# The last tile of a sorted expert layer: 32 rows with float32 weights in column tiles, and a result buffer of its own

## The chip, the core and the metric

One core of a Trainium2 chip runs the program. The metric is device time in microseconds (us) of one execution; lower is better. The engines are named as the profile names them: PE (TensorE), DVE (VectorE), ACT (ScalarE), POOL (GpSimd) and SP (SyncE, which only starts transfers).

## What is computed

Attention over 4 batches, 12 heads, 448 positions and a head width of 64, all float32; its output, 1792 tokens of 768 numbers, goes through a layer of eight experts, of which each token takes the one with the highest logit:

```python
attn_out = _attn_ref(**attn_kwargs)                # causal softmax attention
x = attn_out.transpose(0, 2, 1, 3).reshape(1792, 768)
...
expert_idx = np.argmax(logits, axis=1)             # cosine of x and expert_emb, over tau
gate_w = probs[np.arange(N), expert_idx]
for e in range(8):
    mask = expert_idx == e
    h = np.maximum(x[mask] @ w1[e], 0.0)           # 768 -> 1024
    out[mask] = gate_w[mask, None] * (h @ w2[e])   # 1024 -> 768
```

## The kernel before, in words

The attention runs over 24 pairs of heads in an order written out by hand (`ORDER`, a list of step names with the pair's number). Its last part also sorts the tokens by expert and prepares the expert layer: how many tiles there are, which expert each tile has, which rows it holds.

**Tiles.** The tokens of an expert are cut into tiles of at most 128 rows. The expert with the most tokens comes first, the others follow in their order. With these inputs the experts have 1, 319, 229, 126, 542, 464, 87 and 24 tokens, which makes 18 tiles, numbered 0 to 17. Tiles 0 to 4 are expert 4's, tile 5 expert 0's, 6 to 8 expert 1's, 9 and 10 expert 2's, 11 expert 3's, 12 to 15 expert 5's, tile 16 the 87 rows of expert 6, and tile 17 the 24 rows of expert 7. The program holds 21 tiles (`NT`); from tile 14 (`TMIN`) on, each tile is inside a runtime `If(nt > t)` (L1006, `nt` being the number of tiles), whose `Else` is `last(t - 1)`.

**Flags.** Small integers that a kernel reads into registers at run time tell each engine which form of a tile to run. `small[t]` (read by `load_few`, L574, tested in L584) is 1 for at most 64 rows, 2 for a larger tile of the same expert as the one before, 0 for a larger tile of a new expert. `mt` holds each tile's expert, then a flag that is 1 if the expert changes at this tile (`cc`, read in `val`, L531), then `nt`. Steps U0 to U5 and H0 to H2 (L839 to L876) make them on one partition, among the last steps of `ORDER`.

**Products.** A product in float32 is made of rounded parts: weights are split into a high part (ACT cast, L905) and a low part (DVE subtraction, L906), and so is the token side; a whole tile takes three matmuls for each block (L681 to L683), a tile of at most 64 rows, with high and low token parts side by side in the 128 columns, two (L690, L691). `r1` and `r2` are the weights as loaded, `h1`, `l1`, `h2`, `l2` their parts.

**Order within a tile** (`body(t)`): product 1 of tile t; the split of the next tile's w1 where the expert changes; the loads of w1 for tile t+2; the hidden values of t out of PSUM (`hiddens`); the flags of t+1; tile t+1's tokens turned (`turn_x`, six PE transposes, L623) and split (`next_x`); the gather of tile t+3; product 2 of tile t-1, with the turn of t's hidden values (`turn_h`, eight PE transposes, L632) between its k = 4 and k = 5; the split of w2 for t (L905, L906); `split_h(t)` (the ReLU and the split of the turned values, DVE's part in L670); `finish(t - 1)`; the loads of w2 for t+1. `last(t)` does product 2 of the last tile, two halves of 384 columns one after the other, and `finish`.

**finish** multiplies the two halves by the gate, one half on ACT (L755), one on DVE (L758), into one buffer `ob`, and POOL scatters its rows to the output with an indirect DMA (L766). In a tile of at most 64 rows ACT scales the lower half of the PSUM (L749, by `gu`, a copy of the gates on partitions 64 to 127, made in `upper`), and DVE adds the upper half into `ob` (L752). `ob` is one buffer for all tiles.

**Before the first `body`** come `loads(2, 1)`, which reads flags of tile 2 on SP, ACT, DVE and POOL, and `gate_parts`: ACT takes a square root (L952), DVE refines it (L298 and on), ACT takes an exponential (L962), and POOL makes `Mg` (L975), from which PE makes the gates in tile 1 (`gates`, L986).

The logits use column tiles already: `LT` steps (L449) run three matmuls of 32 columns each (`tile_position`), on 448 columns of data in float32.

Of the kernel before, what the change touches and what calls it, by code (L numbers as in the profile page):

```python
# [18 lines left out]
P = 128  # L19
# [14 lines left out]
K0 = [1, 2, 3, 4, 5, 6, 7, 0]  # L34

# [93 lines left out]
def attn_moe(tc, qk, vv, emb, tau, w1, w2, out):  # L129
# [3 lines left out]
    with ExitStack() as ctx:  # L133
# [51 lines left out]
        junk = T("junk", [DM], BF16)  # L185
# [30 lines left out]
        hh1, ob, xt1, hh0 = (cut(fa, P, n, at=at + o) for n, o in ((F, 0), (DM, F), (DM, F + DM), (F, F + 2 * DM)))  # L216
# [65 lines left out]
        gt, gu = T("gt", [NT], parts=P), T("gu", [NT], parts=P)  # L282
# [228 lines left out]
        for c in range(NC):  # L511
            step(f"Q{c}", LAST)(lambda p, c=c: ac.activation(
                junk, Xs[p // PB % 2][:, c], AF.Square, accum_out=n2[:, NC * (p // PB) + c : NC * (p // PB) + c + 1]))
# [59 lines left out]
        def load_few(t, engines):  # L573
            return nc.values_load(small[0:1, t : t + 1], engines=engines, min_val=0, max_val=2,  # L574
                                  skip_runtime_bounds_check_because="made on chip within these bounds")

        def branch(flag, small_, whole_, light_=None):

            def rest():
                with tc.If(flag > 1) as c:  # L580
                    light_()
                with c.Else():
                    whole_()
            with tc.If(flag == 1) as c:  # L584
                small_()
            with c.Else():
                rest() if light_ else whole_()

        def either(t, engine, small_, whole_, light_=None):

            if t < 2:
                whole_()
            else:
                branch(few[t][engine], small_, whole_, light_)
# [33 lines left out]
        def turn_h(t):  # L628

            def rows():  # L630
                for k in range(KF):
                    pe.transpose(pf[t][k // 4][:, k % 4], hb[t][:, k * P : k * P + P], idt)  # L632
            if t < 2:
                rows()
            else:
                with tc.If(few[t][ET.PE] < 2):
                    rows()

        def turn_light(t):

            blocks = hb[t].rearrange("p (k j c) -> p k j c", k=KF, j=4)

            def light_():
                for q in range(0, P, 32):
                    for j in range(4):
                        v.transpose(xk[32 * j : 32 * j + 32, :, q : q + 32], blocks[q : q + 32, :, j])  # L646
            if t > 1:
                with tc.If(few[t][ET.DVE] > 1):
                    light_()

        def next_x(t, px):
            h, l = ([x[:, 3 * a : 3 * a + 3] for a in range(2)] for x in xs[t][1:])
            for a in range(2):
                ac.copy(h[a], px[a])

            def small_():
                for a in range(2):
                    v.tensor_tensor(h[a][:, :, 64:], px[a][:, :, 0:64], h[a][:, :, 0:64], op=ALU.subtract)

            def whole_():  # L660
                for a in range(2):
                    v.tensor_tensor(l[a], px[a], h[a], op=ALU.subtract)
            either(t, ET.DVE, small_, whole_)

        def split_h(t):
            x, h, l = hs[t]
            pts = [(slice(4 * a, 4 * a + 4), pf[t][a]) for a in range(2)]

            def low(out, x, h):
                v.scalar_tensor_tensor(out, x, 0.0, h, op0=ALU.max, op1=ALU.subtract)  # L670
            either(t, ET.Activation, lambda: [ac.activation(h[:, o, 0:64], pt[:, :, 0:64], AF.Relu) for o, pt in pts],
                   lambda: [ac.activation(h[:, o], pt, AF.Relu) for o, pt in pts], lambda: ac.activation(h, xk, AF.Relu))
            either(t, ET.DVE, lambda: [low(h[:, o, 64:], pt[:, :, 0:64], h[:, o, 0:64]) for o, pt in pts],
                   lambda: [low(l[:, o], pt, h[:, o]) for o, pt in pts], lambda: low(l, xk, h))
# [24 lines left out]
        def product2(t, acc, ks=range(KF), js=(0, 1)):  # L699
            either(t, ET.PE, lambda: small_product(acc, hs[t][1], h2, l2, ks, KF, 384, js),  # L700
                   lambda: product(acc, *hs[t][1:], h2, l2, ks, (K0[0], K0[-1]) if t == 0 else (0, KF - 1), 384, js))

# [24 lines left out]
        def hiddens(t, acc):  # L727

            hs[t] = hb[t] = hh_ring.next()

            def low(j):
                return hb[t][0:64, 512 * j : 512 * j + 512]

            either(t, ET.Activation, lambda: [ac.copy(low(j), acc[j][64:128]) for j in range(2)],
                   lambda: [hidden(t, acc, j) for j in range(2)])
            either(t, ET.DVE, lambda: [v.tensor_tensor(low(j), acc[j][0:64], low(j), op=ALU.add) for j in range(2)],
                   lambda: v.memset(apart, 0.0))
# [3 lines left out]
        def finish(t, acc, ends):  # L741
            def half(j):
# [16 lines left out]

            if ends and t > 1:  # L760
                branch(load_few(t, [ET.DVE, ET.Activation]), lambda: [f(j) for j in range(2) for f in (small_a, small_v)],
                       lambda: (whole_a(), whole_v()))
# [77 lines left out]
        ef, ef2 = T("ef", [NT], parts=1), T("ef2", [NT], parts=1)  # L840
# [17 lines left out]
        same, sa = T("same", [NT], parts=1), T("sa", [NT], parts=1)  # L858

        @step("H0", END)  # L860
        def _(p):
            v.tensor_scalar(sm, us, 1.0 / SKIP, None, ALU.mult)
            v.memset(same, 0.0)

        @step("H1", END)
        def _(p):
            st["f"] = end_ring.next()[:, :NT]
            pe.matmul(st["f"], idt[:, 64:65].broadcast_to([P, P]), sm, start=True, stop=True)
# [39 lines left out]
        def body(t):  # L908
# [6 lines left out]
            if t + 1 < NT:  # L915
                with tc.If(cc[t + 1] != 0):
# [15 lines left out]
            if t > 1:  # L932
                with tc.If(cc[t] != 0):
# [3 lines left out]
            if t > 1:  # L937
                with tc.If(cc[t] != 0):  # L938
# [3 lines left out]
        def last(t):  # L942
            acc = [a[:, :384] for a in acc1]
            for j in range(2):
                product2(t, acc, js=[j])
# [31 lines left out]
        def upper():  # L977

            f = pt_ring.next()[:, :NT]
# [69 lines left out]
```

## Time and profile before

| | |
|---|---|
| median of 3 runs | 509.47 us (509.18 to 509.82) |
| the profiled execution's own time | 508.89 us |
| its span | 507.0 us |
| mean granted clock of PE | 0.994 of full speed |
| PE busy | 490.0 us, 97% of the span |
| DVE / ACT / POOL busy | 349.2 / 337.1 / 72.3 us |

The span is what the profiler sees between the first and the last event; the profiled execution's own time is 1.89 us longer. Attention fills the span up to about 200 us, tiles 0 and 1 and the preparation of the flags and gates the time to about 222 us, the other tiles the rest. Two matmul rows that follow each other overlap in the records, so what a stretch of PE work takes is read from the start of its first row to the start of the next stretch's, not from the rows' durations. The products of tile 17 are the rows of L690 and L691 from 475.82 us (product 1) and from 492.15 us (product 2).

### The profile page before, as it was taken

The page shows a single profiled execution, that of the slowest core. Times are in us where ns is not written, and L with a number is a line of the kernel's source. Part 1 is how long each engine was busy: PE and PEld are TensorE (multiplying, and loading weights), DVE is VectorE, ACT ScalarE, POOL GpSimd, SP SyncE. Part 2 cuts the span into 40 slices and gives each one's busy share as a digit, 9 for nine tenths or more (in the row PEclk, how much of TensorE's full clock was granted, in tenths as well). Part 3 has the DMA queues.
Part 4 walks back from the last instruction along what each step waited for, and adds up shares of the span by engine and source line. Part 5 has one row for each costly group of instructions (what it writes and reads, how often), then busy time and mean ns, then how long its engine had stood idle before and what let it go on. Part 6 is the DMA issues. An engine that isn't in the chain of part 4 may idle for free. (4 is left out here: it accounts for less than half of the span.)

```text
span 507.0 us, 10532 instructions
## 1 busy us (share of the span) xinstructions
PE 490.0 (97%) x3120; PEld 391.1 (77%) x3120; DVE 349.2 (69%) x948; ACT 337.1 (66%) x811; POOL 72.3 (14%) x89
## 2 busy tenths in 40 slices
PE   8999999999999999999999999999999999999992
PEld 5656566666656557888889898899889988988992
DVE  4866585676668568845486986837988554788871
ACT  5999999999999994721255962617676621256660
POOL 2000000000000351230112022200221020012111
PEclk9999999999999999999999999999999999999997
DMA  8232353173235971311449775368677312567831
GB/s 246 67 109 86 126 172 110 58 217 109 63 116 172 343 240 56 95 56 40 174 171 382 262 240 184 141 239 347 255 265 267 129 64 78 237 238 294 274 123 35
DMA packets 27368, 87.19 MB, mean 172 GB/s; under 512 B 2694, under 2 KB 3142, under 8 KB 27280
## 3 DMA queue, kind: packets, MB, share of 16 engines
q1 hardware_dynamic: 24160, 72.38, 41.3%
q0 software_dynamic: 3120, 13.77, 7.6%
q8 instruction: 39, 0.64, 0.5%
q14 instruction: 49, 0.40, 0.2%
HBM read 144.33 MB, written 12.58 MB: 309 GB/s over the span
## 5 line engine op out<-in xcount | busy, mean ns | idle before, releaser
L381 ACT ACTIVATE aq<-aq,mx 112x112 f32<-112x112 f32 (+3 forms) x192 | 99.8, 525 | 4.6 <-DVE mx L376 4.6
L376 DVE CUSTOM_DVE_ANT_0 aq<-bank,ar 112x112 f32<-112x112 f32 (+1 forms) x192 | 76.1, 441 | 30.5 <-PE bank L371 30.1
L399 PE MATMUL bank<-idt,aq 112*112 112x112 f32 x480 | 62.3, 265 | 1.1 <-DVE ap L404 0.4
L399 PEld LDWEIGHTS bank<-idt,aq 112*112 112x112 f32 x480 | 46.7, 133 | 19.5 <-ACT ap L404 6.8
L371 PE MATMUL bank<-ak 64*112 64x112 f32 (+3 forms) x384 | 56.6, 419 | 0.8 <-DVE mx L376 0.8
L725 ACT COPY fa<-bank 128x512 f32<-128x512 f32 x28 | 15.2, 587 | 56.6 <-PE bank L681 48.0
L766 POOL DMA_INDIRECT out_dram<-fa,isx x18 | 26.4, 1469 | 183.5 <-DVEq L938 60.0
L404 ACT COPY ap<-bank 112x336 f32<-112x336 f32 (+2 forms) x118 | 50.4, 457 | 2.7 <-PE bank L399 0.8
L412 PE MATMUL bank<-ap 112*64 112x448 f32 (+3 forms) x384 | 51.7, 407 | 0.0
L906 DVE TENSOR_TENSOR wl<-fa,wh 128x1024 fp32r<-128x1024 f32 x42 | 48.4, 1219 | 3.6 <-PE bank L682 2.1
L646 DVE STREAM_TRANSPOSE turned<-fa 32x256 f32<-32x256 f32 x112 | 48.8, 436 | 1.5
L412 PEld LDWEIGHTS bank<-ap 112*64 112x64 f32 x384 | 25.0, 136 | 29.9 <-issue 17.6
L905 ACT CAST wh<-fa 128x1024 fp32r<-128x1024 f32 x42 | 40.7, 1047 | 4.4 <-PE bank L683 2.0
L371 PEld LDWEIGHTS bank<-ak 64*112 64x112 f32 x384 | 27.4, 175 | 13.0 <-issue 3.5
L381 ACT ACTIVATION_READ_ACCUMULATOR aq<-aq,mx 112x1 f32 x192 | 37.1, 193 | 0.0
L565 POOL DMA_INDIRECT fa<-xd,ig x21 | 23.5, 1117 | 75.9 <-PE bank L623 54.6
L681 PE MATMUL bank<-wh,akr 128*128 128x512 f32 x84 | 32.9, 391 | 0.0
L683 PE MATMUL bank<-wh,akr 128*128 128x512 f32 x84 | 32.9, 391 | 0.0
L683 PE MATMUL bank<-wh,apr 128*128 128x512 f32 x84 | 32.8, 391 | 0.0
L682 PE MATMUL bank<-wl,aor 128*128 128x512 f32 x84 | 32.8, 390 | 0.0
L682 PE MATMUL bank<-wl,akr 128*128 128x512 f32 x84 | 32.8, 390 | 0.0
L681 PE MATMUL bank<-wh,aor 128*128 128x512 f32 x84 | 32.8, 390 | 0.0
(292 smaller groups left out, 1061.1 us busy)
## 6 DMA issues: line engine op xcount, KB each, us to landing
fa<-in_w_dram SPq DMA_DIRECT2D x76, 768.0 KB
fa<-in_w_dram SPq DMA_DIRECT2D x54, 1024.0 KB
ak<-in_qk_dram SPq DMA_DIRECT2D x24, 448.0 KB
ap<-in_vv_dram SPq DMA_DIRECT2D x24, 224.0 KB
xd<-fa SPq DMA_DIRECT2D x3, 1344.0 KB
fa<-in_w_dram SPq DMA_DIRECT2D x6, 512.0 KB
xd<-fa SPq DMA_DIRECT2D x1, 1120.0 KB
fa<-xd,ig POOLq DMA_INDIRECT x21, 6.4
```

The lines of the kernel that those rows point to most:

```text
L371: pe.matmul(o, raws[p % 4][rows, 0, CP * i : CP * i + CP], raws[p % 4][rows, 1, :n], start=True, stop=True, tile_position=(D * h, 0), skip ...
L376: v.tensor_tensor_reduce(out=Ps[p % 2][i, h], in0=st.pop(("sp", p, i, h)), in1=mask[i], scale=-0.125, scalar=3e38, op0=ALU.add, op1=ALU.mi ...
L381: ac.activation(x, x, AF.Exp, bias=mxs[p % 3][:, h, i : i + 1], scale=-1.0, accum_out=sums[p % 3][:, h, i : i + 1])
L399: pe.transpose(t[:, x, c], Ps[p % 2][i, h][:, c * CP : c * CP + CP], idt[:CP, :CP])
L404: (ac.copy if q == "A" and (p, n) not in ONV else v.tensor_copy)(o, st.pop(("pt", p, n)))
L412: pe.matmul(bo[64 * h : 64 * h + 64, CP * c : S], vts[p % 4][:, c, 64 * h : 64 * h + 64], PTs[p % 2][:, h, 4 * c : 3 * c + NC], start=c == ...
L646: v.transpose(xk[32 * j : 32 * j + 32, :, q : q + 32], blocks[q : q + 32, :, j])
L681: pe.matmul(acc[j], xh[:, k], wh[k][:, o], start=k == ends[0], stop=False)
L682: pe.matmul(acc[j], xh[:, k], wl[k][:, o], start=False, stop=False)
L683: pe.matmul(acc[j], xl[:, k], wh[k][:, o], start=False, stop=k == ends[1])
L905: ac.copy(h[k], r[:, k])
L906: v.tensor_tensor(l[k], r[:, k], h[k], op=ALU.subtract)
```

## The change

The flag `small` gets a value 3: the last tile, if its expert is new and it has at most 32 rows. Such a tile's weights are not split; both products use them as loaded, in float32, with the token side's 32 columns as stationary operand and the weight's columns in four quarters, each on 32 PE columns of its own. `cc` gets a value 2 for it, by which the splits are skipped and the loads are not. The last tile writes its result into the next buffer of the ring for gathered tokens, whatever its form. `junk` goes; its steps write into a part of another buffer. `hq` and `gq` are new, `xq` is the old `en`.

```diff
-        junk = T("junk", [DM], BF16)
...
+        gt, gu, gq = T("gt", [NT], parts=P), T("gu", [NT], parts=P), T("gq", [NT], parts=P)
+        hq, xq = T("hq", [KF, QR], parts=P), en.rearrange("p k r -> p k r")
...
         def turn_h(t):
...
-                with tc.If(few[t][ET.PE] < 2):
+                with tc.If(few[t][ET.PE] < 2) as c:
                     rows()
+                if t >= TMIN:
+                    with c.Else():
+                        with tc.If(few[t][ET.PE] > 2):
+                            rows(KF // NQ)
...
         def next_x(t, px):
...
+            def tiny_():
+                for a in range(2):
+                    v.tensor_copy(xq[:, 3 * a : 3 * a + 3], px[a][:, :, 0:QR])
+            either(t, ET.DVE, small_, whole_, tiny_=tiny_)
...
         def split_h(t):
...
+                   lambda: ac.activation(hq.rearrange("p (q b) r -> p b q r", q=NQ),
+                                         pf[t][0][:, 0 : KF // NQ].rearrange("p b (q r) -> p b q r", q=NQ), AF.Relu))
...
+                   lambda: v.memset(apart, 0.0))
...
+        def tiny_product(acc, x, w, nk, n):
+
+            for k in range(nk):
+                for q in range(NQ):
+                    pe.matmul(acc[0][QR * q : QR * q + QR, :n], x[:, k], w[:, k, n * q : n * q + n], start=k == 0,
+                              stop=k == nk - 1, tile_position=(0, QR * q), skip_group_check=True)
...
         def product1(t, acc):
             either(t, ET.PE, lambda: small_product(acc, xs[t][1], h1, l1, range(KD), KD, 512),
-                   lambda: product(acc, *xs[t][1:], h1, l1, range(KD), (0, KD - 1), 512))
+                   lambda: product(acc, *xs[t][1:], h1, l1, range(KD), (0, KD - 1), 512),
+                   tiny_=lambda: tiny_product(acc, xq, r1, KD, F // NQ))
...
+            either(t, ET.PE, small_, whole_, tiny_=lambda: tiny_product(acc, hq, r2, KF, DM // NQ))
...
         def finish(t, acc, ends):
+            ob = xt_ring.next() if ends else obs
+
...
+            def quarters(qs, f):
+                n = DM // NQ
+                for q in qs:
+                    rows = slice(QR * q, QR * q + QR)
+                    f(ob[0:QR, n * q : n * q + n], acc[0][rows, :n], gq[rows, t : t + 1])
+
+            def tiny_():
+                quarters((0, 1), lambda o, x, s: ac.activation(o, x, AF.Copy, scale=s))
+                quarters((2, 3), lambda o, x, s: v.tensor_scalar(o, x, s, None, ALU.mult))
...
         @step("U5", END)
         def _(p):
-            v.tensor_tensor(mt[:, NT + 1 : 2 * NT], ef[:, 1:NT], ef[:, 0 : NT - 1], op=ALU.not_equal)
-            v.tensor_copy(mt[:, 2 * NT : 2 * NT + 1], ct[0:1, E - 1 : E])
+            nt = ct[0:1, E - 1 : E]
+            v.tensor_tensor(ch[:, 1:], ef[:, 1:NT], ef[:, 0 : NT - 1], op=ALU.not_equal)
+            v.scalar_tensor_tensor(ch, i21[0:1], nt, ch, op0=ALU.is_lt, op1=ALU.mult)
+            v.tensor_copy(mt[:, NT + 1 : 2 * NT], ch[:, 1:])
+            v.tensor_copy(mt[:, 2 * NT : 2 * NT + 1], nt)
+            v.tensor_scalar(lt, i21[0:1], 1.0, nt, ALU.add, ALU.is_equal)
...
         @step("H2", END)
         def _(p):
-            f = st["f"]
-            v.tensor_tensor(same[:, 1:], ef[:, 1:NT], ef[:, 0 : NT - 1], op=ALU.is_equal)
-            v.tensor_tensor(sa, f[0:1], same, op=ALU.mult)
-            v.tensor_tensor(same, same, sa, op=ALU.subtract)
-            v.scalar_tensor_tensor(small, same, 2.0, f[0:1], op0=ALU.mult, op1=ALU.add)
+            f, q = (st["f"][0:1, n * NT : n * NT + NT] for n in range(2))
+            v.tensor_tensor(lt, lt, q, op=ALU.mult)
+            v.tensor_scalar(sa, ch, -1.0, 1.0, ALU.mult, ALU.add)
+            v.scalar_tensor_tensor(sa, f, 0.0, sa, op0=ALU.is_equal, op1=ALU.mult)
+            v.tensor_tensor(sa, sa, lt, op=ALU.add)
+            v.scalar_tensor_tensor(small, sa, 2.0, f, op0=ALU.mult, op1=ALU.add)
+            v.tensor_tensor(mt[:, NT + 1 : 2 * NT], ch[:, 1:], lt[:, 1:], op=ALU.add)
...
-                cc[t] = val(NT + t, 1, [ET.SP, ET.Activation, ET.DVE, ET.Pool])
+                cc[t] = val(NT + t, 2, [ET.SP, ET.Activation, ET.DVE, ET.Pool])
...
         def body(t):
...
-                with tc.If(cc[t + 1] != 0):
+                with tc.If(cc[t + 1] == 1):
                     split_w(r1, h1, l1, range(KD))
...
-                with tc.If(cc[t] != 0):
+                with tc.If(cc[t] == 1):
                     split_w(r2, h2, l2, range(6))
...
         def upper():
...
+            for q in range(NQ):
+                pe.matmul(fq[QR * q : QR * q + QR], idt[:, 0:QR], gt, start=True, stop=True, tile_position=(0, QR * q),
+                          skip_group_check=True)
+            v.tensor_copy(gq, fq)
```

`branch` and `either` get a fourth form (tested by `flag > 2`, only for tiles from 14 on), H0 has a multiplication in place of a memset, H1 a second small matmul, `hiddens` a form in which ACT copies 128 by 256 values, and both halves of product 2 in `last` come under one test instead of two.

## Rows read from the trace of the kernel before

**Rows 1.** The page's first part: busy time and share of the span, by engine.
```profile
PE 490.0 (97%) x3120; PEld 391.1 (77%) x3120; DVE 349.2 (69%) x948; ACT 337.1 (66%) x811; POOL 72.3 (14%) x89
```
**Rows 2.** Stretches of the end: length, busy time by engine, granted clock, DMA share, GB/s.
```profile
491.40:498.20 6.80, 5.96 (x32) 5.51 (x32) 3.19 (x6) 2.33 (x4) 1.82 (x1) 1.00 0.17 55
498.20:507.00 8.80, 0.00 (x0) 0.00 (x0) 1.13 (x2) 0.58 (x1) 1.00 (x1) 0.65 0.03 11
```
**Rows 3.** Waits of PE from 222 to 507 us: total, times, longest.
```profile
PE bank L690 <- DVE aor L670: 0.8, 1, 0.8
```
**Rows 4.** Timeline of PE, tiles 16 and 17: start, duration, instruction, idle time before it.
```profile
475.82 0.39 PE L690 MATMUL bank<-wh,aor 128*128 128x512 f32 x1
...
481.30 0.82 PE L623 MATMUL bank<-idt,fa 128*128 128x128 f32 x6
...
487.17 1.04 PE L632 MATMUL bank<-idt,fa 128*128 128x128 f32 x8
487.96 0.42 PE L681 MATMUL bank<-apr,arr 128*128 128x384 f32 x1
...
492.15 0.41 PE L690 MATMUL bank<-arr,aor 128*128 128x384 f32 x1 [0.79 <-DVE aor L670]
```
**Rows 5.** Timeline of DVE, the two calls of finish and what stands before the first.
```profile
491.58 0.75 DVE L670 SCALAR_TENSOR_TENSOR aor<-bank,aor 128x256 fp32r<-128x256 f32 x2
492.24 0.61 DVE L758 TENSOR_SCALAR fa<-bank,gt 128x384 f32<-128x384 f32 x1
...
499.85 1.13 DVE L752 SCALAR_TENSOR_TENSOR fa<-bank,gt,fa 64x384 f32<-64x384 f32 x2 [5.26 <-DMA out_dram<-fa,isx]
```
**Rows 6.** Timeline of POOL: the scatters of tiles 16 and 17.
```profile
493.66 1.82 POOL L766 DMA_INDIRECT out_dram<-fa,isx  x1 [10.30 <-ACT apr L905]
501.79 1.00 POOL L766 DMA_INDIRECT out_dram<-fa,isx  x1 [6.32 <-POOLq L1006]
```
**Rows 7.** The line of the scatters, 470 to 507 us: durations in ns, first and last start.
```profile
L766 POOLq EVENT_SEMAPHORE  x3: 2014/6475/6782, 471.8 to 499.0; - x3
...
DMA to landing us min/median/max: 2.4/5.3/7.1
```
**Rows 8.** Column tiles in the attention: PE's timeline, and one line's groups.
```profile
101.11 0.95 PE L449 MATMUL bank<-ao,en 128*32 128x448 f32 x6
101.99 0.31 PE L399 MATMUL bank<-idt,aq 112*112 112x112 f32 x1
...
L449 PEld LDWEIGHTS bank<-ao,en x48: 106/108/109, 33.0 to 189.4; 128*32 128x32 f32 x48
```
**Rows 9.** Jumps of the sequencers by line, 485 to 495 us (L584: from 200 us).
```profile
L1006 PEldq COMPARE_BRANCH  x1: 3292/3292/3292, 488.1 to 488.1; - x1
L584 PEldq COMPARE_BRANCH  x38: 63/208/352, 222.4 to 478.6; - x38
...
L1006 ACTq COMPARE_BRANCH  x1: 50/50/50, 491.6 to 491.6; - x1
L574 ACTq TENSOR_LOAD <-small x1: 277/277/277, 494.8 to 494.8; - x1
```
**Rows 10.** The flags and the gates, 209 to 221 us: a flag load by line, then timelines.
```profile
L531 ACTq TENSOR_LOAD <-mt x1: 467/467/467, 209.4 to 209.4; - x1
...
210.23 1.28 ACT L952 ACT_TABLE_LOAD   x1 [0.34 <-issue]
...
212.03 0.17 DVE L876 SCALAR_TENSOR_TENSOR small<-same,bank 1x21 int32<-1x21 f32 x1
212.74 0.17 DVE L298 TENSOR_SCALAR t<-t 112x16 f32<-112x16 f32 x1 [0.55 <-DVE small L876]
...
216.75 2.48 POOL L975 TENSOR_TENSOR Mg<-M,g 112x336 f16<-112x336 f16 x3 [6.20 <-DVE g L969]
...
220.30 0.67 PE L986 MATMUL bank<-Mg,turned 112*128 112x63 f16 x16
```
**Rows 11.** The line of the weight loads on SP, about 480 us: the last load for tile 17.
```profile
L893 SPq DMA_DIRECT2D fa<-in_w_dram x1: 372/372/372, 480.0 to 480.0; - x1
```

More of the change, by code (lines that the diff above doesn't have):

```diff
@@ L34 @@
 K0 = [1, 2, 3, 4, 5, 6, 7, 0]
+QR = 32
+NQ = P // QR
 ORDER = """
@@ L573, in load_few, with branch @@
         def load_few(t, engines):
-            return nc.values_load(small[0:1, t : t + 1], engines=engines, min_val=0, max_val=2,
+            return nc.values_load(small[0:1, t : t + 1], engines=engines, min_val=0, max_val=3,
                                   skip_runtime_bounds_check_because="made on chip within these bounds")
-        def branch(flag, small_, whole_, light_=None):
+        def branch(flag, small_, whole_, light_=None, tiny_=None):
             def rest():
+                if not light_:
+                    return whole_()
                 with tc.If(flag > 1) as c:
@@ L583, in rest, with more @@
                     whole_()
+            def more():
+                if not tiny_:
+                    return rest()
+                with tc.If(flag > 2) as c:
+                    tiny_()
+                with c.Else():
+                    rest()
             with tc.If(flag == 1) as c:
@@ L586, in branch, with either @@
             with c.Else():
-                rest() if light_ else whole_()
-        def either(t, engine, small_, whole_, light_=None):
+                more()
+        def either(t, engine, small_, whole_, light_=None, tiny_=None):
             if t < 2:
@@ L593, in either @@
             else:
-                branch(few[t][engine], small_, whole_, light_)
+                branch(few[t][engine], small_, whole_, light_, tiny_ if t >= TMIN else None)
         def xT(t, a):
@@ L628, in turn_h, with rows @@
         def turn_h(t):
-            def rows():
-                for k in range(KF):
+            def rows(n=KF):
+                for k in range(n):
                     pe.transpose(pf[t][k // 4][:, k % 4], hb[t][:, k * P : k * P + P], idt)
@@ L647, in turn_light @@
             if t > 1:
-                with tc.If(few[t][ET.DVE] > 1):
+                with tc.If(few[t][ET.DVE] == 2):
                     light_()
@@ L734, in hiddens @@
             either(t, ET.Activation, lambda: [ac.copy(low(j), acc[j][64:128]) for j in range(2)],
-                   lambda: [hidden(t, acc, j) for j in range(2)])
+                   lambda: [hidden(t, acc, j) for j in range(2)],
+                   tiny_=lambda: ac.copy(hb[t][:, : F // NQ], acc[0][:, : F // NQ]))
             either(t, ET.DVE, lambda: [v.tensor_tensor(low(j), acc[j][0:64], low(j), op=ALU.add) for j in range(2)],
@@ L862, in _ @@
             v.tensor_scalar(sm, us, 1.0 / SKIP, None, ALU.mult)
-            v.memset(same, 0.0)
+            v.tensor_tensor(lt, lt, ch, op=ALU.mult)
         @step("H1", END)
         def _(p):
-            st["f"] = end_ring.next()[:, :NT]
-            pe.matmul(st["f"], idt[:, 64:65].broadcast_to([P, P]), sm, start=True, stop=True)
+            st["f"] = end_ring.next()
+            for n, row in enumerate((64, QR)):
+                pe.matmul(st["f"][:, n * NT : n * NT + NT], idt[:, row : row + 1].broadcast_to([P, P]), sm, start=True,
+                          stop=True, skip_group_check=True)
         @step("H2", END)
         def _(p):
-            f = st["f"]
-            v.tensor_tensor(same[:, 1:], ef[:, 1:NT], ef[:, 0 : NT - 1], op=ALU.is_equal)
-            v.tensor_tensor(sa, f[0:1], same, op=ALU.mult)
-            v.tensor_tensor(same, same, sa, op=ALU.subtract)
-            v.scalar_tensor_tensor(small, same, 2.0, f[0:1], op0=ALU.mult, op1=ALU.add)
+            f, q = (st["f"][0:1, n * NT : n * NT + NT] for n in range(2))
[5 more added lines that the diff above has]
+            v.tensor_tensor(mt[:, NT + 1 : 2 * NT], ch[:, 1:], lt[:, 1:], op=ALU.add)
         for _ in range(16):
@@ L943, in last @@
             acc = [a[:, :384] for a in acc1]
-            for j in range(2):
-                product2(t, acc, js=[j])
+            product2(t, acc)
             finish(t, acc, True)
```

34 lines of the change are left out of this document (20 added, 14 removed).

## Prediction

> **What bounds the kernel now.** The page's first part comes first: PE is busy 97% of the span [rows 1]. Such a share says nothing yet of a change at the end, so the second view is the table of stretches: PE is full up to 491.4, has an idle part up to 498.2, and in the last 8.8 us no instruction at all; there it is two DVE calls, one ACT call, one POOL call and waiting [rows 2]. The third is the waits of PE from 222 us on: the only one worth naming is the 0.8 us on DVE before product 2 of the last tile [rows 3]. So from 222 to 492 us every us of PE work, and every us by which PE starts late, goes straight to the end. The timelines then give the end as a chain. PE's last product of tile 16 gives way at 491.36 (0.79 before 492.15 [rows 4]); DVE does the second half of `finish(16)` at 492.24, 0.88 late because L670 sits ahead of it [rows 5]; POOL starts the scatter at 493.66, 0.81 after DVE's end at 492.85 [rows 5, 6]; it lands 5.3 us later, at 499.0, which is when the last semaphore wait of the scatters' line begins [rows 7]. DVE waits for that landing, 5.26 us, because `ob` is one buffer, and runs only from 499.85 to 500.98 [rows 5]; the last scatter starts at 501.79 and lands 2.4 us later, near 504.2 [rows 6, 7]; the span ends 2.8 us after. Product 2 of tile 17, over by 498.2 [rows 2], isn't in this chain: the first scatter's landing is.
>
> The same rows show that POOL itself waits for the scatter before: its three semaphore waits of 2.0 to 6.8 us stand in the line of the scatters, and one begins at the landing just named [rows 7]. A second buffer takes away DVE's wait, but I keep POOL's: the two scatters write the same output.
>
> **Part by part, PE before the end.** Product 1 of tile 17 takes 475.82 to 481.30, 5.48 us for 24 matmuls of 512 columns [rows 4]. It becomes 24 float32 matmuls of 256 columns on four column tiles. The nearest rows are three column tiles of 448 columns in float32: six instructions for three calls, so two passes, and 101.11 to 101.99 = 0.88 us for both [rows 8]. If the three ran one after another, each call of 448 columns would have 0.29 us for two passes, less than one pass of a whole-array product of 512 columns scaled to 448 (5.48 / 24 x 448 / 512 = 0.20, twice is 0.40). So tiles do run side by side. Per column and pass it is at most 0.88 / 896 = 0.98 ns; part of that is the start of a stretch, and I take 0.85 ns and 0.24 us once. Six k by two passes by 256 columns by 0.85 ns, and 0.24, is about 2.83 us. The gain is **2.65 us**. The bounds: 0.75 ns (gain 2.9), and four tiles in place of three at a proportional price (4/3 x 0.98 ns x 3072 = 4.0, gain 1.5).
>
> `turn_h(17)` does two transposes in place of eight; eight take 487.17 to 487.96, 0.79 us [rows 4], so **0.59 us** go. Both lie in PE's full stretch. Product 2 of tile 16 then ends at 491.36 - 3.24 = 488.12.
>
> **The end.** With no split for tile 17, neither L670's part nor a weight split stands ahead of `finish(16)` on DVE: it starts at about 488.2 and ends at 488.81 (0.61 [rows 5]), POOL starts at 489.62, the scatter lands at 494.94 (5.3 [rows 7]). That is 4.04 earlier. POOL then starts the last scatter 0.81 after that landing, at 495.75, if its data are there; before, the DVE call and its waits stood between (501.79 - 499.0 = 2.8 from landing to start), so another 2.0 go. 495.75 + 2.45 + 2.76 gives 500.96 in place of 507.0: **6.05 us**.
>
> The data must be there by 494.9. Product 2 of tile 17 is 8 k x 2 passes x 192 columns at 0.85 ns, 2.6 and start-up, 2.7 us; its 64 matmuls with as many weight loads issue in that time if they go as fast as the 16 of L986, 0.67 us for 16, 42 ns each [rows 10]. It starts after PE's jump to the `Else`. That jump took 3.29 us, where 38 others of L584 took 0.06 to 0.35 [rows 9]; PE's sequencer reached it 3.3 us ahead of the engine, so it was hidden, and it moves with the work: start near 488.65, end 491.35. ACT's own jump lasted from 491.6 to the flag's load at 494.8 [rows 9], 3.2 us. It moves by PE's 3.2, to 488.4, and is over near 491.6; DVE's, begun when its part of `finish(16)` ends at 488.81, would by the same length be over near 492.0. With the flag's load and two quarters on each engine (half of a 0.61 each, say 0.3) the data are there near 493.0 to 493.3. The slack is **1.6 us**; in it lie the last product's size, the six transposes fewer and the ReLU, which move nothing.
>
> The Trainium skill ("Runtime: NRT & Kernel Launch", section "Instruction fetch mechanics") says that a taken branch whose target lies outside the window of two pages forces a fetch by DMA before execution goes on; the 3.29 us against 0.06 to 0.35 agree. By that page a fourth form in the code adds targets, and a second such jump could stand on the last chain; it is rival B.
>
> **The price, at the flags.** H2 now ends with a write to the `cc` flags, which ACT reads for tile 2 before its square root. Before, that load ran at 209.4, while DVE was still at the flags until 212.20 [rows 10]; the table load, 1.28 us from 210.23, and the root, some 0.2, followed, and DVE went on at 212.74. After, ACT's load waits for H2's last operation. U5 has three more small operations, H0 a multiplication instead of a memset, H2 two more, at 0.17 to 0.2 each [rows 10]: H2 ends near 213.0 (212.20 + 0.8; bounds 0.5 to 1.2). From the load's start at 209.4 to the root's end is 2.35 us; from 213.0 it ends at 215.35, and DVE's L298 moves from 212.74 to 215.4, 2.65 later. The chain behind it (ACT's exponential, `Mg` on POOL) moves along: `Mg` ends at 216.75 + 2.48 + 2.65 = 221.88 in place of 219.23. PE began the gates at 220.30, straight after other work, so 1.07 of it is slack [rows 10]: PE starts them near 221.95, **1.65 us later**, and from there nothing on PE is idle until 491, so it arrives whole at the end. Bounds: 1.2 to 2.1, and 0 if the load's wait is finer than I think. H1's second matmul and the flag loads of the other engines lie under that. The four small matmuls in `upper` are PE work: **0.2 us** (eight instructions at the 42 ns of L986 are 0.34, less what overlaps).
>
> Edits at nothing: the squares written elsewhere (same operation, same size); the two copies of `next_x` and the one of `hiddens`, on DVE and ACT, in place of more work there; the loads, which stay, so SP's queue keeps its order. Both products now read the loaded weights themselves. The last w2 load for tile 17 is issued at 480.0 [rows 11], before anything on PE has moved, and is wanted for the last two k, after 490: ten us, where the slowest scatter took 7.1 [rows 7]. POOL's queue holds nothing behind the last scatter, and what was behind ACT's and DVE's splits, `finish(16)`, is counted above.
>
> **Sum.** -6.05 + 1.65 + 0.2 = -4.2 us. The profiled execution, 508.89, would become 504.7; the median stands 0.58 above it, so **505.3 us**.
>
> **Rivals.** A: the flag load isn't delayed (it waits for U5's write alone). Then the 1.65 doesn't come: 503.7. Against it: the load reads the same cells that H2's last operation writes.
>
> B: a second long jump, as long as the one of 3.29 us, on ACT's, DVE's or PE's way to the last quarters. Less the slack of 1.6 it costs 1.7, less some overlap 1.4: 506.7. For it: four forms lie in the code where three did. Against: all jumps of L584 on PE were short [rows 9].
>
> C: weight loads of column tiles aren't hidden. One takes 106 ns [rows 8]; one more on each of product 1's 12 passes is 1.3 us, and on product 2's 16 passes 1.7, which uses up the slack and 0.1 more: 506.7. Against it: with 448 columns two passes with their six loads fit in 0.88 [rows 8], which leaves little beside the columns themselves. The skill ("TensorE: Matmul & The Clock Gate", Part 3, "The mechanism") says that a weight load overlaps matmuls in flight only where the row group differs, which speaks against this change, since all four tiles share the rows; by that rule the sum is C's, and the 0.88 us speaks against it.
>
> D, the slower side: the four column tiles run one after another. Place: the two tiny products. Price: product 1 is 4 x 2.6 + 0.24 = 10.6 in place of 5.48, +5.2, where -2.65 was counted, so all before the end moves by 7.8; product 2 is 10.4, 7.7 longer than counted, less 1.6 of slack, 6.1. 505.3 + 7.8 + 6.1 is 519. It decides from about 2.1 rounds for each pass: 2.6 a round for product 1 and as much for product 2, less 1.6, then eat the 4.2. Against it: three tiles did run together [rows 8]; only a fourth is untried in these rows.
>
> E: the last tile doesn't take the tiny form, and only the buffer changes. ACT and DVE then finish the two halves behind product 2, which is over by 498.2, by about 499.4; POOL starts at 500.2 in place of 501.79, 1.6 gained, 1.85 paid: 509.7. Against: 24 rows, a new expert, the last of 18 tiles.
>
> **Chances.** Forecast 0.6, A 0.14, B 0.08, C 0.08, D 0.05, E 0.05. A measurement of this kernel can tell about 0.2%, 1.0 us, from no change. Faster by more than that hold the forecast, A, B and C, 0.9; same E, 0.05; slower D, 0.05. The forecast's own terms reach from -6.2 (product 1 at 0.75 ns, price at 1.2) to -2.6 (product 1 at 4.0, price at 2.1), of which the far ends together are unlikely. The range of 8 in 10 takes in B and C above and most of the way to A below: **503.0 to 507.8**.
>
> **What would show it.** After the change: (1) the products of tile 17 with 32-column weights, product 1 near 2.8 us from its start to the next row's; (2) no wait of DVE for the output's DMA, and POOL's last semaphore wait beginning at the landing of scatter 16, about 7 us after `finish(16)`'s DVE call starts; the last scatter 0.8 after it; (3) PE idle for 1.5 to 1.7 us before L986's successor, with ACT's table load near 214; (4) one jump over 3 us on each engine, none after it. Wrong would be: PE's two products longer than 4 us (C or D), the last scatter waiting for ACT or DVE (B), no idle time of PE before the gates (A), or a split for tile 17 (E).

## The result, and the profile after

The median went from 509.36 us (509.18 to 509.82) to **504.38 us** (504.26 to 505.32, 4 runs each): a ratio of 0.9905, 95% interval 0.9888 to 0.9922. Another chip gave 0.9906 (0.9885 to 0.9927). The forecast was 505.3. The profiled execution took 504.50 (forecast 504.7), its span is 502.7 in place of 507.0.

PE's timeline of the changed kernel, from tile 17's product 1 to its product 2 (lines have moved: L690 and L691 are now the L721 of the tiny products, L623 is L636, L632 is L645, L681 to L683 are L705 to L707):

```profile
477.56 2.80 PE L721 MATMUL bank<-fa,en 128*32 128x256 f32 x48
480.29 0.87 PE L636 MATMUL bank<-idt,fa 128*128 128x128 f32 x6
...
486.43 0.38 PE L645 MATMUL bank<-idt,fa 128*128 128x128 f32 x2
486.56 0.42 PE L705 MATMUL bank<-apr,arr 128*128 128x384 f32 x1
...
489.60 0.34 PE L707 MATMUL bank<-apr,aqr 128*128 128x384 f32 x1
491.08 3.33 PE L721 MATMUL bank<-fa,hq 128*32 128x192 f32 x64 [1.14 <-DVE fa L800]
```

Product 1 holds PE for 480.29 - 477.56 = 2.73 us instead of 5.48 [rows 4]; the turn for 486.56 - 486.43 = 0.13 instead of 0.79. The last full product gives way at 489.94, 1.42 earlier than before. Then PE stands idle for 1.14 before the last product, where it stood 0.79. The row names DVE's L800, which ends just there, at 491.06, but it is PE's jump (below) that holds it. In every profile in which `last` is reached by a jump, the kernel before and the experiments included, the last product begins 0.7 to 0.8 us after the jump's end, while the end of L800 lies anywhere from 1.1 us before that begin to just at it.

The timelines of ACT, DVE and POOL at the end (`finish` of tile 16 is L797 and L800, of tile 17 L809 and L810):

```profile
489.76 0.58 ACT L797 ACTIVATE fa<-bank,gt 128x384 f32<-128x384 f32 x1 [1.42 <-PE bank L705]
494.50 0.85 ACT L809 ACTIVATE fa<-bank,gq 32x192 f32<-32x192 f32 x2 [4.16 <-PE bank L721]
...
490.44 0.62 DVE L800 TENSOR_SCALAR fa<-bank,gt 128x384 f32<-128x384 f32 x1 [5.72 <-ACTq L999]
495.44 0.87 DVE L810 TENSOR_SCALAR fa<-bank,gq 32x192 f32<-32x192 f32 x2 [4.39 <-ACT fa L809]
...
491.87 1.02 POOL L818 DMA_INDIRECT out_dram<-fa,isx  x1 [8.99 <-DVEq L999]
497.46 1.00 POOL L818 DMA_INDIRECT out_dram<-fa,isx  x1 [4.58 <-POOLq L1071]
```

DVE no longer waits for the output's transfer [rows 5]. The line of the scatters and that of the runtime test:

```profile
L818 POOLq EVENT_SEMAPHORE  x3: 17/43/5097, 486.0 to 496.6; - x3
...
DMA to landing us min/median/max: 2.8/3.8/4.8
...
L1071 PEldq COMPARE_BRANCH  x1: 3719/3719/3719, 486.7 to 486.7; - x1
```

Scatter 16 starts at 491.87, lands 4.8 us later at 496.6, where POOL's last wait begins (before: 499.0 [rows 7]), and the last scatter follows 0.8 behind. PE's jump to `last` takes 3.72 us and ends at 490.4.

The span's 4.3 us, stretch by stretch; each is a difference of times in [rows 2, 4, 6, 7] and in the rows above:

| stretch | before | after | gain | forecast |
|---|---|---|---|---|
| start to product 1 of tile 17 | 475.82 | 477.56 | -1.74 | -1.85 |
| from there to the end of product 2 of tile 16 | 15.54 | 12.38 | 3.16 | 3.24 |
| to the start of scatter 16 | 2.30 | 1.93 | 0.37 | 0.80 |
| to its landing | 5.3 | 4.8 | 0.5 | 0 |
| to the start of the last scatter | 2.8 | 0.8 | 2.0 | 2.0 |
| to the end of the span | 5.2 | 5.2 | 0 | 0 |

The first line holds the price at the flags, in timelines of ACT, DVE, POOL and PE:

```profile
213.14 1.28 ACT L1012 ACT_TABLE_LOAD   x1 [3.61 <-DVE mt L937]
...
212.36 0.16 DVE L937 TENSOR_TENSOR mt<-ch,lt 1x20 int32<-1x20 f32 x1
214.68 0.17 DVE L300 TENSOR_SCALAR t<-t 112x16 f32<-112x16 f32 x1 [2.16 <-ACT t L1012]
...
218.70 2.48 POOL L1035 TENSOR_TENSOR Mg<-M,g 112x336 f16<-112x336 f16 x3 [8.02 <-DVE g L1029]
...
221.23 0.67 PE L1051 MATMUL bank<-Mg,turned 112*128 112x63 f16 x16 [0.85 <-POOL Mg L1035]
...
233.10 0.29 PE L1041 MATMUL bank<-gt,idt 128*64 128x21 f32 x2
233.67 0.26 PE L1044 MATMUL bank<-gt,idt 128*32 128x21 f32 x8 [0.28 <-DVE gu L1042]
234.05 0.85 PE L636 MATMUL bank<-idt,fa 128*128 128x128 f32 x6
```

ACT waits 3.61 us for H2's last operation, POOL is done 1.95 later than before [rows 10], and PE stands 0.85 before the gates. In `upper` PE waits once more, 0.28, for DVE's copy of `gu`. The turn behind it starts 1.65 later than in the kernel before, whose row is

```profile
232.40 0.87 PE L623 MATMUL bank<-idt,fa 128*128 128x128 f32 x6
```

### The profile page after: what moved, and what is told of

Same layout as the page of the kernel before. It is cut to its first block, busy times and chain, and to the rows that moved or that the text cites. A ratio compares the mean times of both kernels' runs of the same rounds, so it can differ in the third digit from the quotient of the medians.

```text
span 502.7 us, 10651 instructions
## 1 busy us (share of the span) xinstructions
PE 484.6 (96%) x3180; PEld 384.1 (76%) x3180; DVE 334.0 (66%) x939; ACT 323.9 (64%) x795; POOL 69.7 (14%) x89
## 5 line engine op out<-in xcount | busy, mean ns | idle before, releaser
L818 POOL DMA_INDIRECT out_dram<-fa,isx x18 | 24.1, 1341 | 180.7 <-DVEq L999 55.8
L967 DVE TENSOR_TENSOR wl<-fa,wh 128x1024 fp32r<-128x1024 f32 x36 | 41.5, 1220 | 3.1 <-PE bank L706 1.6
L966 ACT CAST wh<-fa 128x1024 fp32r<-128x1024 f32 x36 | 34.9, 1047 | 3.5 <-PE bank L707 1.6
L705 PE MATMUL bank<-wh,akr 128*128 128x512 f32 x84 | 32.9, 391 | 0.0
L707 PE MATMUL bank<-wh,akr 128*128 128x512 f32 x84 | 32.9, 391 | 0.0
L707 PE MATMUL bank<-wh,apr 128*128 128x512 f32 x84 | 32.9, 391 | 0.0
L705 PE MATMUL bank<-wh,aor 128*128 128x512 f32 x84 | 32.8, 390 | 0.0
```

The lines of the kernel that those rows point to most:

```text
L705: pe.matmul(acc[j], xh[:, k], wh[k][:, o], start=k == ends[0], stop=False)
L707: pe.matmul(acc[j], xl[:, k], wh[k][:, o], start=False, stop=k == ends[1])
L966: ac.copy(h[k], r[:, k])
L967: v.tensor_tensor(l[k], r[:, k], h[k], op=ALU.subtract)
```

## The experiments

All ratios are to the kernel before on the same chip; the changed kernel's own, on two chips, are 0.9905 and 0.9906.

**The flags.** H2's last operation writes only the flags that a tiny tile can have:

```diff
-            v.tensor_tensor(mt[:, NT + 1 : 2 * NT], ch[:, 1:], lt[:, 1:], op=ALU.add)
+            v.tensor_tensor(mt[:, NT + TMIN : 2 * NT], ch[:, TMIN:], lt[:, TMIN:], op=ALU.add)
```

> H2's last operation writes the flags of tiles 14 to 20 only, so that the load of tile 2's flag on ACT no longer has to wait for it. Theory: the wait of PE for Mg, 0.85 us before the gates in the profile of the changed kernel, is all due to that load; ACT's table load for the root is back near 210.3, PE goes from the turn to the gates without a gap, and the time falls by 0.85 to 0.95, to 503.5. Rival 1, the forecast's figure: the price is 1.65, the time 502.7. Rival 2: DVE's longer H2 (0.3 us later) and the operations behind it hold Mg as long, and the time falls by less than 0.3, to 504.1 or more.

Measured: 503.77, ratio 0.9886 (0.9868 to 0.9903), about 0.97 less than the changed kernel by the ratios. Timelines of ACT and PE:

```profile
210.03 1.28 ACT L1012 ACT_TABLE_LOAD   x1
...
220.00 0.82 PE L636 MATMUL bank<-idt,fa 128*128 128x128 f32 x6
220.65 0.67 PE L1051 MATMUL bank<-Mg,turned 112*128 112x63 f16 x16
```

No wait of ACT, none of PE. The interval overlaps that of the changed kernel, so the time alone doesn't settle it; the trace does: the gap before the gates was all due to this one load.

**upper.** The same, and the two copies behind all five matmuls:

```diff
             pe.matmul(f[64:128], ...)
-            v.tensor_copy(gu[64:128], f[64:128])
             for q in range(NQ):
                 pe.matmul(fq[QR * q : QR * q + QR], ...)
+            v.tensor_copy(gu[64:128], f[64:128])
             v.tensor_copy(gq, fq)
```

> The flags edit of c_flags_first, and in upper all five small matmuls ahead of the two copies, so that the four new ones no longer wait for DVE's copy of gu (0.28 us in the profile of the changed kernel). Theory: of the 0.72 us by which tile 2 falls back at upper, the wait and the start of a second group go, 0.3 to 0.4; with the flags 1.2 to 1.3 us less than the changed kernel. Rival: the 0.72 is the eight instructions themselves, and only the flags' 0.9 is gained.

Measured: 503.51, ratio 0.9874 (0.9853 to 0.9895), beside 505.23 of the changed kernel on this chip: 1.7 less, somewhat more than the theory's 1.2 to 1.3. Its PE timeline there:

```profile
233.01 0.29 PE L1041 MATMUL bank<-gt,idt 128*64 128x21 f32 x2
233.23 0.26 PE L1043 MATMUL bank<-gt,idt 128*32 128x21 f32 x8
```

The four small matmuls now follow at once; in the last experiment's timeline below they take 0.19 us, so of the 0.72 by which tile 2 fell back (0.93 at the gates, 1.65 at the next turn), 0.5 was the wait and its restart.

**The own buffer, from both sides.** First the kernel before with nothing but the buffer, then the changed kernel without it:

```diff
         def finish(t, acc, ends):
+            ob = xt_ring.next() if ends else obs
...
-            ob = xt_ring.next() if ends else obs
+            ob = obs
```

> The kernel before with a buffer of its own for the last tile and nothing else. Theory: DVE's wait of 5.26 us goes, its second call ends near 499.4, 0.6 after ACT's second half, and POOL starts near 500.2 in place of 501.8: 1.5 to 1.6 less, 507.8. Rival 1: POOL's wait for the landing (499.0) takes its place and DVE's calls don't matter, 2.0 less, 507.4. Rival 2: nothing is gained, 509.4.

> The changed kernel with the last tile's result in the buffer of all other tiles. Theory: the quarters on ACT, then on DVE, wait for the landing of scatter 16 (496.6), take 0.85 and 0.87 one after the other, and POOL needs its 0.81 behind them: the last scatter starts 1.7 to 1.8 later, 506.1 to 506.2. Rival: POOL waits for that landing anyway, so the own buffer is worth nothing, 504.4.

Measured: 508.53 against 510.10 on that chip, ratio 0.9965 (0.9951 to 0.9978), 1.6 to 1.8 less, the theory's figure (the interval holds rival 1's 2.0 as well; in the trace the data come last, by 0.3: POOL's wait begins at the landing, 499.9, and lasts 0.298 us); and 506.03, ratio 0.9922 (0.9908 to 0.9935), 0.8 more than the changed kernel by the ratios, half of what was expected, with overlapping intervals. The timeline of DVE in the first, and of ACT in the second:

```profile
497.93 0.61 DVE L754 SCALAR_TENSOR_TENSOR fa<-bank,gt,fa 64x384 f32<-64x384 f32 x1 [2.62 <-issue]
499.53 0.61 DVE L754 SCALAR_TENSOR_TENSOR fa<-bank,gt,fa 64x384 f32<-64x384 f32 x1 [0.99 <-ACT fa L751]
```

```profile
496.60 0.85 ACT L809 ACTIVATE fa<-bank,gq 32x192 f32<-32x192 f32 x2 [5.41 <-DMA out_dram<-fa,isx]
```

With one buffer ACT waits for the landing, as the theory has it. But product 2 ends at 495.76 there, so the quarters could have begun only 0.8 earlier.

**Column tiles.** All k of a quarter first, then the next quarter:

```diff
-            for k in range(nk):
-                for q in range(NQ):
+            for q in range(NQ):
+                for k in range(nk):
```

> The loops of the tiny products swapped: all k of one quarter, then the next, so that matmuls that follow each other lie on the same column tile. Theory (the four tiles of a pass run side by side): the work is the same, but the four quarters now come one after another; product 1 goes from 2.73 to about 10.5, product 2 from 3.3 to about 10.4, of which 0.4 is slack: 504.4 + 7.8 + 6.7 = 519. Rival (rival C's kind: the passes are bound by weight loads or issue, not by columns): both products keep within a factor of two, under 510.

Measured: 515.2 (515.1 to 515.3, 2 runs), ratio 1.0106. The theory holds in kind, but product 1 takes 8.0 and not 10.5. PE's timeline, then that line's stretches, one inside a quarter and one at its end (length, PE busy with the number of matmuls in flight, weight loads, clock, DMA share, GB/s):

```profile
478.21 8.05 PE L721 MATMUL bank<-fa,en 128*32 128x256 f32 x48
486.19 0.87 PE L636 MATMUL bank<-idt,fa 128*128 128x128 f32 x6
```

```profile
478.50:479.50 1.00, 1.00 (x6) 0.50 (x5) 1.00 0.87 262
480.00:480.80 0.80, 0.80 (x9) 0.49 (x8) 1.00 1.03 399
```

and the same measure in product 1 of the changed kernel:

```profile
478.20:479.20 1.00, 1.00 (x25) 0.62 (x20) 1.00 0.86 241
```

Inside a quarter 6 matmuls touch one us, with four tiles in turn 25: one column tile takes the time that four take together. At the end of a quarter it is 9 in 0.8 us: there the last matmuls of one quarter run beside the first of the next. That is what the expectation missed. 36 steps in 8.0 us, 0.22 each, are four pairs at each of three changes, and the starts of the single matmuls in the trace show these twelve pairs.

**The data or the landing.** The forecast gave the last scatter's data 1.6 us of slack. Quarters 2 and 3 of the last product in a second PSUM bank, so that DVE needn't wait for ACT (above, 4.39 <-ACT fa L809):

```diff
-                    pe.matmul(acc[0][QR * q : QR * q + QR, :n], ...)
+                    pe.matmul(acc[q * banks // NQ][QR * q : QR * q + QR, :n], ...)
...
-                    f(ob[0:QR, n * q : n * q + n], acc[0][rows, :n], gq[rows, t : t + 1])
+                    f(ob[0:QR, n * q : n * q + n], acc[q // 2][rows, :n], gq[rows, t : t + 1])
```

and ACT's and DVE's halves of every `finish` under one test:

```diff
-                either(t, ET.Activation, lambda: [small_a(j) for j in range(2)], whole_a)
-                either(t, ET.DVE, lambda: [small_v(j) for j in range(2)], whole_v)
+                either(t, "AV", lambda: [f(j) for j in range(2) for f in (small_a, small_v)], lambda: (whole_a(), whole_v()))
```

> The changed kernel as it is, on the same chip as the next three, as their reference: 0.99 of the kernel before.

> The changed kernel with quarters 2 and 3 of the last product in a second PSUM bank, so that DVE's two calls run beside ACT's instead of behind them: data for the last scatter 0.85 us earlier. Theory: scatter 16's landing (496.65) comes 0.3 after the data (496.31), so at the most nothing to 0.1 us is gained. Rival: the last scatter waits for its data, and the time falls by 0.8.

> The changed kernel with ACT's and DVE's half of finish under one test, so that DVE's half no longer waits for the end of ACT's: in finish(16) it could start at 490.05, when PE is done, in place of 490.44. Theory: scatter 16 starts and lands 0.39 earlier, then the data are last; 0.3 to 0.4 us less. Rival: the landing isn't what the end hangs on, or the wait for ACT is replaced by another; 0.

Measured on one chip: the changed kernel 505.23 (0.9906), two banks 504.08 (0.9890, 0.9869 to 0.9912), one test 505.67 (0.9918, 0.9896 to 0.9940). My theory lost both times. The rival of the first, 0.8 less, is near the measured 0.8 to 1.2 (the intervals overlap). The second gained nothing, though scatter 16 did start 0.39 sooner after PE's last full product (1.54 in place of 1.93). Timelines of DVE with two banks, of PE and POOL with one test:

```profile
495.81 0.86 DVE L810 TENSOR_SCALAR fa<-bank,gq 32x192 f32<-32x192 f32 x2 [4.17 <-PE bank L721]
...
491.80 2.47 PE L721 MATMUL bank<-fa,hq 128*32 128x192 f32 x52 [1.86 <-SPq L1071]
...
491.48 1.02 POOL L817 DMA_INDIRECT out_dram<-fa,isx  x1 [7.75 <-DVEq L999]
```

With two banks DVE no longer waits for ACT. With one test L800 ends 0.4 us earlier, yet PE still stands 1.86 before its last product, so L800 isn't what it waits for. The changed kernel's profile on this chip shows what was last; timelines of PE, DVE and POOL, the scatters' line, the jump:

```profile
492.64 2.47 PE L721 MATMUL bank<-fa,hq 128*32 128x192 f32 x52 [1.89 <-DVEq L999]
495.40 0.84 PE L721 MATMUL bank<-fa,hq 128*32 128x192 f32 x12 [0.29 <-issue]
...
497.29 0.86 DVE L810 TENSOR_SCALAR fa<-bank,gq 32x192 f32<-32x192 f32 x2 [5.42 <-ACT fa L809]
...
498.96 1.00 POOL L818 DMA_INDIRECT out_dram<-fa,isx  x1 [5.27 <-POOLq L1071]
```

```profile
L818 POOLq EVENT_SEMAPHORE  x3: 17/1607/3154, 488.8 to 496.6; - x3
...
L1071 PEldq COMPARE_BRANCH  x1: 4479/4479/4479, 487.5 to 487.5; - x1
```

Scatter 16 has landed at 496.6, and POOL's wait goes on for 1.607 us, until DVE's quarters end at 498.15. The jump took 4.48 us here and PE stood 1.89 after its last full product. In the first profile the landing was last by 0.3 (DVE's end 496.31, landing 496.6); here the data by 1.6, and with one test by 1.6 too, so that a scatter 16 that starts earlier could gain nothing. Of the 1.9 us between the two profiles the longer idle time of PE makes 0.75 (1.89 against 1.14), a pause within product 2 another 0.3, and the landing the largest part: it took 3.9 us here and 4.8 there. So the two ends are close, and the jump and the landing together settle which is last.

What the jump meets differs too. Transfers on all queues while PE's last jump lasts: the kernel before, the changed kernel on this chip, and g_quarters_outer, where tile 17 came late:

```profile
DMA packets 1, 0.02 MB, mean 5 GB/s; under 512 B 0, under 2 KB 0, under 8 KB 0
DMA packets 191, 0.72 MB, mean 160 GB/s; under 512 B 41, under 2 KB 41, under 8 KB 188
DMA packets 2, 0.02 MB, mean 7 GB/s; under 512 B 0, under 2 KB 0, under 8 KB 0
```

The three jumps took 3.29, 4.48 and 3.70 us. The last weight loads and POOL's transfers are over before the jump in the first and the third, and run beside it in the second. They do so in all other profiles of the changed kernel and its variants that jump to `last`, too: the jump took 3.72 us in the first profile, with 0.32 MB beside it, and 3.96 to 4.44 in the others.

**The jump itself.** `last(t - 1)` first, so that it is reached without one:

```diff
-            keep = hs[t - 1]
-            with tc.If(nt > t) as c:
-                body(t)
-                rest(t + 1)
-            hs[t - 1] = keep
-            with c.Else():
-                last(t - 1)
+            with tc.If(nt < t + 1) as c:
+                last(t - 1)
+                xt_ring.n -= 1
+            with c.Else():
+                body(t)
+                rest(t + 1)
```

> The changed kernel with the two sides of the runtime test exchanged: last(t - 1) stands first, in the If, and body(t) in the Else, so that the end is reached without a jump. Theory: PE's jump of 3.7 to 4.5 us ahead of product 2 goes, which PE shows as 1.1 to 1.9 us between its last full product and the tiny one; the gap falls to 0.3 to 0.6, ACT's and DVE's flag loads come 2 us earlier, the data are no longer last, and the last scatter starts 0.81 after the landing in every profile: 0.3 to 1.0 less than the changed kernel. Rival: tiles 14 to 17 now jump over the code of last on every engine, up to four times, and what sticks out beyond the 3.3 us by which PE's sequencer is ahead shows as idle time of PE: 0.5 to 4 us more.

Measured: 513.65, ratio 1.0074 (1.0050 to 1.0098). The rival won: the timeline of PE at the end, then the jumps of PE's sequencer from 430 us on, and PE's waits.

```profile
499.33 2.81 PE L721 MATMUL bank<-fa,hq 128*32 128x192 f32 x64
```

```profile
L597 PEldq COMPARE_BRANCH  x6: 326/3334/5714, 439.0 to 487.1; - x6
```

```profile
PE bank L705 <- ACT aor L693: 3.3, 1, 3.3
PE bank L705 <- DVEq L665: 2.0, 1, 2.0
PE bank L705 <- DVEq L994: 1.3, 1, 1.3
```

The gap before the last product is gone, and product 2 is down to 2.81. Yet from the end of the last full product (499.40) to the end of the span it is 12.7 us, where the changed kernel's first profile has 12.8 (the second 13.4), so the theory's gain isn't shown. And other jumps, 3.3 us in the median and up to 5.7, now stand in tiles 14 to 17, on a line that had none above 0.35 before [rows 9]. The three waits for ACT and DVE beside them add up to 6.6 us of PE, more than the rival's 4; the kernel is some 8.6 slower than the changed one by the ratios, and where the rest goes is open.

**The splits kept.** `tc.If(cc[...] != 0)` again in place of `== 1` at all three places.

> The changed kernel with the splits of tile 17's weights made all the same (tests for not 0 instead of 1), though nothing reads them. Theory: they lie on ACT and DVE ahead of finish(16) and of the last quarters as in the kernel before: scatter 16 starts 0.8 to 1.2 later, the last quarters near 497 on DVE; 1.0 to 1.4 more than the changed kernel. Rival: PE and the landing hide them, 0 to 0.2 more.

Measured: 505.93, ratio 0.9919 (0.9897 to 0.9942): 0.7 more than the changed kernel by the ratios, less than the theory and with overlapping intervals, so the size is open. The scatters' line shows a part that nobody had named:

```profile
L818 POOL DMA_INDIRECT out_dram<-fa,isx x2: 997/1406/1815, 492.8 to 499.7; - x2
...
DMA to landing us min/median/max: 3.1/4.6/6.1
```

**Together.** All edits, with `last` first; then flags, upper and two banks alone.

> All edits together: the flags of tiles 14 to 20 alone in H2's last operation, the five small matmuls of upper in one go, two PSUM banks for the last product, ACT's and DVE's half of finish under one test, and last ahead of body. Theory: 1.2 from the flags and upper, 0.4 from finish(16), and the data never last: 1.8 to 2.5 less than the changed kernel, a ratio of 0.986 to 0.987 to the kernel before. Rival: the jumps over last eat it, as in l_last_first.

> The three edits that gained by themselves, without the exchange of the sides and without the single test: the flags of tiles 14 to 20 alone in H2's last operation, the five small matmuls of upper in one go, two PSUM banks for the last product. Theory: the first two act before tile 3 and the third at the end, so they add up: about 1.6 (c2_flags_upper against the changed kernel) and 0.4 to 0.9 for the data, which were last by 0.2 to 1.6 in most profiles; 2.0 to 2.5 less than the changed kernel, a ratio of 0.986 to the kernel before. Rival: the landing of scatter 16 is last once the data come earlier, so the banks add nothing: 0.987.

Measured: 511.83 (1.0039, 1.0022 to 1.0057), where the jumps eat all; and 503.32 (0.9884, 0.9864 to 0.9905). Against 0.9874 for flags and upper alone, the banks' share can't be seen: the intervals cover each other. The theory's 0.986 lies outside the last interval, the rival's 0.987 within it. The timeline of PE in the last one:

```profile
232.44 0.26 PE L1043 MATMUL bank<-gt,idt 128*32 128x21 f32 x8
232.63 0.87 PE L636 MATMUL bank<-idt,fa 128*128 128x128 f32 x6
```

By the medians both this and c2_flags_upper are shorter than the changed kernel; of c2_flags_upper, which ran on the same chip, even the longest run, 504.00, lies below the changed kernel's shortest, 504.36.

## Why the prediction was right, and where it wasn't

The size and the sign came from the steps named: product 1's 2.65 (2.75 measured), the turn's 0.59 (0.66), the 2.0 from landing to last scatter. The price per column of four tiles, 0.85 ns, held: product 1's 12 passes of 256 columns took 2.73 us with their start, 0.89 ns a column, or 0.81 less the 0.24 put down for the start. Rival D fell with product 1 (10.6 by its price), and g_quarters_outer shows the tiles of a pass side by side. A fell with ACT's wait for H2's last operation, E with the rows of 32 columns in both products. C fell with product 1: a weight load of 0.106 more for each pass would have made it 4.0. By the Trainium skill ("TensorE: Matmul & The Clock Gate", Part 3, "The mechanism"), loads overlap only across row groups; the 25 matmuls in 1 us, each with a load of its own, on one row group, speak against that for column tiles.

Four steps were off, and they partly cancelled, which is luck. So is part of the rest: in the profiled execution the forecast is 0.2 off (504.7, measured 504.50), and in the median 0.9, since it put the median 0.58 above the profiled execution and it came 0.12 below.

- The price at the flags: 1.65 + 0.2 forecast, 0.93 + 0.72 measured. "H2 ends near 213.0" was the step that failed in the first: it ended at 212.52, 0.32 later than before in place of 0.8. That is 0.48 of the 0.72 missing; another 0.22 is the way from there to the root's end, 2.13 (to 214.65) in place of 2.35. The mechanism (the load waits for H2, `Mg` is late) is shown by c_flags_first. In the second the instructions were right (0.19 in the timeline above), but the wait for DVE's copy in front of them was overlooked.
- "so it was hidden, and it moves with the work", said of PE's jump: in the kernel before it ended at 491.4, just as PE's last full product did, so there was no slack left in it. It starts 3.3 us ahead of PE's end as before, but took 3.7 to 4.5 us, and PE stood 1.1 to 1.9. So product 2 began at 491.08, where PE's measured end and the forecast's 0.53 would give 490.47. The jump moved with the work, and the last weight loads didn't: they now run beside it.
- "two quarters on each engine (half of a 0.61 each, say 0.3)": two take 0.85, and DVE's come behind ACT's, since both read one PSUM bank; with a second bank the wait is gone (j_two_banks), and the time is 0.8 to 1.2 less, with overlapping intervals. Product 2, put at 2.7, took 3.33. Of the slack of 1.6 the late start of product 2 took 0.6 and its length 0.6, and some 0.3 was left; in the next profile it was -1.6. From product 2's end to the data the forecast had 1.65 to 1.95, mostly for jumps of ACT and DVE, and 1.9 was measured (494.41 to 496.31), mostly for quarters one behind the other: the right size by luck. Rival B was right about the place, with 0.4 to 1.2 us of a longer first jump in place of a second one.
- That DVE starts `finish(16)` "at about 488.2" counted for 0.8, of which 0.37 came: DVE's half of `finish(16)` waits for ACT's (490.34 is ACT's end, 490.44 DVE's start). In its place came 0.5 from a quicker landing of scatter 16, which nothing in the forecast had.

Three readings in the prediction are wrong by themselves and change nothing above. If the three calls of [rows 8] ran one after another, 0.29 us would be more than one pass (0.20), not less; what counts is that it is less than the two passes' 0.40. At 0.85 ns a column the 0.88 us of that row leave 0.12 for the start of a stretch, not 0.24. And the near end of the forecast's terms, 0.75 ns and a price of 1.2, adds up to -4.9, not -6.2.

What stays open is the jump's length. The jumps with transfers beside them were the longer ones, 3.7 to 4.5 us; without any they took 3.29 in the kernel before, 3.34 in the one with the buffer alone, and 3.70 in the changed kernel with the quarters one after another. That the transfers lengthen it is argued from this; no experiment varied them alone, and the 0.4 that remain are unexplained.

## What to carry to other kernels

When the chain at the end is a store that waits for a store, what counts is when the first one starts; a buffer of its own helps the second only down to that landing, and the data then have to be as early. A flag that is written again late delays everyone who reads any of the cells written, so late writes should cover only the cells that need them. Before one gives a rare form its own code, one should ask which jumps get longer: in these runs the jump to the far side of a runtime test took 2.5 to 5.7 us wherever it was put, free only where the sequencer was as far ahead.

## What was not expected of the hardware

- Matmuls on different column tiles overlap even when they stand several places apart: with the quarters one after another, 48 matmuls of 256 columns took 8.0 us instead of the 10.5 that 0.22 each would make.
- The scatter of a full tile kept POOL 1.82 us and landed after 5.3 with DVE at work on a split at the same time [rows 6, 7], 1.02 and 4.8 in the changed kernel with DVE idle (3.4 to 4.8 over its variants), and 1.81 and 6.1 again with the splits kept. That DVE's work is the cause is argued from these runs; none varied it alone, and it isn't enough by itself: the changed kernel's scatter at 480.58 kept POOL 1.02 with DVE at a split all the while (479.69 to 481.57).
